# Turning batch 0's last three attention tiles on TensorE, and holding batch 1's first stacks behind tile 45

## The chip, the cores and the metric

The kernel runs on one core of a Trainium2 chip. The metric is device time in microseconds (us); the kernel before takes 764.54 us, the median of 3 runs (763.83 to 765.95). The engines are named as in the profile: PE (TensorE, its weight loads shown apart as PEld), DVE (VectorE), ACT (ScalarE), POOL (GpSimd) and SP (SyncE, which issues nearly all DMAs here).

## The reference

Three layers follow each other on a batch of 2, a sequence of 768 and a width of 512 (8 heads of 64).

```python
q_bucket, k_bucket = sums of 2**i over the signs of q @ proj, k @ proj   # 6 bits
scores = np.where(q_bucket == k_bucket, q @ k.T / 8, -1e9)
attn = softmax(scores) @ v                                # layer 1, per head
u = x + real(fft2(x)); un = (u - mean) / sqrt(var + 1e-6)
x = u + relu(un @ w_ch1) @ w_ch2                          # layer 2, hidden width 2048
theta = x @ w_theta
u = x + w_tok_r @ (x * cos(theta)) + w_tok_i @ (x * sin(theta))
out = u + relu(u @ w_ch)                                  # layer 3
```

## The kernel before

**Tiles.** Attention works on tiles of 128 queries by 768 keys. Each batch has 48 of them: 4 pairs of heads, 2 heads, 6 tiles of queries. For one tile PE makes the scores into PSUM (`pss`), DVE takes the row maximum (`nm`), ACT the exponential (`p`), then `p` is split into a high and a low half-precision part, turned so that keys lie on the partitions, and multiplied on PE with the values into `pso`. A head's six tiles done, DVE divides by the sums and writes the head's columns of `x` (the "norm").

**Two ways to turn a tile.** In way "d" POOL splits `p` (`attn_split`, L387) and a DMA transposes the parts (`transposed`, L410). In way "p" PE transposes the unsplit tile with six matmuls against the identity (`turn_pe`, L394), and ACT and DVE split it on the way out of PSUM (`split_turned`, L401: two ACT and two DVE instructions of 128x384). In batch 0 the two alternate, `pet='dp'`: even tiles go by "d", odd ones by "p".

**Order.** Batch 0's attention (`attention_first`, L472) is written out step by step: step n takes tile n's exponential, tile n+1's maximum, tile n-1's PE transposes and so on. While it is traced, `Ordered.keep` chains every instruction to the one before it on its engine; those instructions carry L64 in the profile. All others carry L62, and a list scheduler places them by priority, `at(us)`, and by its own estimate of time. Each engine then runs its list strictly in that order.

**What else runs.** `prep` (L235) makes a head pair's "stacks": it loads q, k and v (`tt`, `vr`), scales k on POOL, splits v (`vv`: an ACT copy, then DVE), splits q and k (`stk`: ACT copies, POOL differences, DMAs between partitions), and adds the bucket bits by two small matmuls, DVE signs and ACT copies. Beside attention, `conv16` (L173) turns w_ch1 (`w1h`, `w1l`) and w_ch2 (`w2h`, `w2l`) from 64-bit integers into two half-precision parts, 16 pieces each: a load into one of three buffers `r`, two ACT passes, one DVE pass, an ACT copy (high part), a POOL difference (low part). As batch 0's heads end, `fold` (L579) begins the Fourier transform on DVE and ACT (`fa`, `zraw`, `hl...`); `rest` finishes it on PE (`psm` from `ct`, `sn`, `dt`), `ln_first` (L725) normalizes its first two row tiles (`un`, turned on PE into `unT`), and the hidden layer of batch 0 starts (`mlp1`: `psm<-unT,w1h`; `mlp2`: `psm<-w2h,hh`), in three groups of 256 rows. Batch 1's attention (`attention`, L435) runs meanwhile; in it all tiles go by "d", with ACT or POOL for the high part. After its last head come batch 1's transform, norm and hidden layer, then layer 3 of both.

**Gates.** `after_gate` (L428) makes what is traced inside it stand behind a given instruction. The edge is one of order, on that instruction's own engine alone. `gate["p1"]` holds batch 1's first `prep`; in the kernel before it is the row maximum, on DVE, of tile `c1` = 32.

Of the kernel before, what the change touches and what calls it, by code (L numbers as in the profile page):

```python
# [70 lines left out]
def fused_kernel(ctx, tc, A, out):  # L71
    nc = tc.nc
    V, AC, PE, PL, SY = (Ordered(tc, e) for e in (nc.vector, nc.scalar, nc.tensor, nc.gpsimd, nc.sync))
# [13 lines left out]
    def stt(eng, out, in0, in1, op, scale=1.0):  # L87
# [5 lines left out]
    T = dict(  # L93
        pet='dp', dup=1, c2=0, c0=44, cx=0, wm=6, gf=1, o2=0, xs=1, sb=2, al=[['p', 2], ['p2', 3], ['pt', 3]], cs='v', g0=1,
        lg=[[0, 2], [2, 4], [4, 6]], ub=2, pace0=1.6, lead=60, f0=60.0, w1=60.0, w1s=1.0, b1=115, pace1=2.6,
        w2=100.0, w2s=1.0, m0=170.0, f1=190.0, th=240.0, m1=290.0, z0=330.0, wt=300.0, n1=16, k1=16, c1=32,
        ne=42, es=150, ld='ss', lc='s', ps=[[0, 3], [0, 5], [1, 0], [1, 5]])
    P3 = ((0, 0), (0, 1), (1, 0))

# [26 lines left out]
    def at(us):  # L126

        tc.cur_priority = int(1000 * us)
# [94 lines left out]
    gate, made = {}, {}  # L223
# [151 lines left out]
    def attn_max(ps):  # L375
        nm = mk(sm_p, [128, 1], F32, "nm")
        return nm, V.tensor_reduce(out=nm, in_=ps[:, :, 0:384], axis=AX.XY, op=ALU.max, negate=True)
# [94 lines left out]
    def attention_first(pace, after):  # L472

        x_t[0] = mk(x_p, [128, NT, DM], F32, "x")
        N = 8 * NT
        ps, nm, ex, p, p2, tp, pt, o = ({} for _ in range(8))
# [23 lines left out]
        nm[0], _ = attn_max(ps[0])  # L500
        for n in range(N + 7):
            at(pace * n)
            m, kind = n % 12, lambda i: T["pet"][i % 2] if 0 <= i < N else ""
            if n < N:
                scores(n + 1)
                p[n], e = attn_exp(ps.pop(n), nm[n])
# [3 lines left out]
            if n + 1 < N:  # L510
                nm[n + 1], x = attn_max(ps[n + 1])
                if n + 1 == T["c1"]:
                    gate["p1"] = [x]
                if n + 1 == T["c0"]:
                    gate["cv"] = [x, e]
            if n - 1 in tp:
# [241 lines left out]
    w1, w2 = {}, {}  # L758
# [129 lines left out]
    h1, l1, c1, c2 = (ev(k) for k in ("aapap", "p", "p", "p"))  # L888
# [4 lines left out]
    with after_gate("start"):  # L893
        ft0 = Fft(0, "left")

    attention_first(T["pace0"], lambda b, j: ft0.fold(PO[j]))
    al = [x for t in kept for x in one(t, *range(t.shape[1]))]
    for k, n in T["al"]:
# [206 lines left out]
```

## Time and profile before

| | |
|---|---|
| median of 3 runs | 764.54 us |
| profiled execution | 762.63 us |
| its span on the core | 760.9 us |
| PE busy, share of the span | 676.1 us, 89% |
| DVE / ACT / POOL busy | 444.2 / 400.0 / 370.5 us |

The profiled execution took 1.73 us more than its span, the time around the first and the last instruction, and 1.91 us less than the median of the runs. Times in the rows are microseconds from the start of the span. A row of the timeline gives start, length, engine, line, operation, output and input tiles with their shapes, how many instructions were merged into it, and in brackets how long the engine sat idle before it and what ended the wait. Names are without buffer numbers, so `w1h`, `w1l`, `p`, `pt` can be memory that a tile of attention borrows from the weights' room.

### The profile page before, as it was taken

How to read it: one execution, taken by the hardware profiler on the slowest of the kernel's cores; microseconds unless marked ns; L12 is line 12 of the kernel's file. 1: busy time of each engine (PE TensorE's matmuls, PEld its weight loads, DVE VectorE, ACT ScalarE, POOL GpSimd, SP SyncE). 2: the span in 40 equal slices, each digit the busy share in tenths (PEclk: the TensorE clock that was granted, in tenths of full speed). 3: DMA queues.
4: the chain of work that ended last, by engine and by line, in shares of the span. 5: the costliest groups of instructions: out<-in, count | busy, mean ns of one | idle time of the engine just before them, and what ended most of it. 6: DMA issues, size and time to landing. Idle time of an engine off the chain costs nothing.

```text
span 760.9 us, 14094 instructions
## 1 busy us (share of the span) xinstructions
PE 676.1 (89%) x5684; PEld 533.2 (70%) x5684; DVE 444.2 (58%) x728; ACT 400.0 (53%) x629; POOL 370.5 (49%) x296
## 2 busy tenths in 40 slices
PE   6978687778397898999989979999999998899997
PEld 2766566566295654786777666687584988899997
DVE  6778878698889755742395861154422496422222
ACT  4787596966597788773222161164325674730000
POOL 4786777896675888875460200033303378320000
PEclk7899996959599999999999989999999999799999
DMA  9675777678687999878640270020005612431100
GB/s 319 147 162 111 167 126 154 137 204 192 173 187 148 258 233 255 149 148 124 104 171 0 59 150 1 1 56 15 1 1 167 195 55 73 164 126 56 56 29 28
DMA packets 152641, 93.23 MB, mean 123 GB/s; under 512 B 126272, under 2 KB 138752, under 8 KB 152576
## 3 DMA queue, kind: packets, MB, share of 16 engines
q1 hardware_dynamic: 150704, 85.87, 48.5%
q0 software_dynamic: 1872, 6.47, 2.4%
q8 instruction: 44, 0.72, 0.4%
q14 instruction: 21, 0.17, 0.1%
HBM read 49.62 MB, written 6.29 MB: 73 GB/s over the span
## 4 chain that ended last, share of the span: by engine, by line
PE 44%; DVE 19%; DMA 11%; ACT 10%; issue 9%; POOL 7%; SPq 0%; POOLq 0%; ACTq 0%; DVEq 0%
PE psm L62 28%; PE psf L62 8%; DMA pt<-p 3%; PE pss L64 2%; ACT r L62 2%; DVE fa L64 2%; DVE nm L64 2%; DVE r L62 2%; DVE t L62 2%; PE pss L62 2%; DMA r<-in_wtok 2%; DMA r<-in_w 2%; DVE fa L62 1%; DVE rr L62 1%; ACT stk L64 1%
## 5 line engine op out<-in xcount | busy, mean ns | idle before, releaser
L62 PE MATMUL psm<-unT,w1h 128*128 128x256 f16 x768 | 131.9, 276 | 8.2 <-DMA unT<-u 4.8
L62 PE MATMUL psm<-unT,w1l 128*128 128x256 f16 x384 | 105.8, 276 | 0.0
L62 PEld LDWEIGHTS <-w1h 128*128 128x128 f16 (+1 forms) x774 | 75.6, 99 | 24.8 <-issue 12.1
L62 DVE SCALAR_TENSOR_TENSOR r<-r 128x512 uint32<-128x512 uint32 x58 | 57.6, 995 | 53.0 <-ACT r L62 48.2
L64 PE MATMUL pss<-stk 128*128 128x384 f32 x192 | 52.5, 397 | 23.6 <-ACT p L64 7.8
L62 PEld LDWEIGHTS <-hh 128*128 128x128 f16 x384 | 37.1, 99 | 43.1 <-issue 2.7
L62 DVE TENSOR_REDUCE nm<-pss 128x1 f32<-128x768 f32 x48 | 45.1, 950 | 34.6 <-PE pss L62 34.6
L62 ACT ACTIVATE r<-r,chalf 128x512 uint32<-128x512 uint32 x58 | 44.4, 766 | 35.7 <-DMA r<-in_wtok 16.7
L62 PE MATMUL psm<-w2l,hh 128*128 128x512 f16 x192 | 61.0, 383 | 0.0
L62 PE MATMUL psm<-w2h,hl 128*128 128x512 f16 x192 | 60.9, 382 | 0.0
L62 DVE SCALAR_TENSOR_TENSOR hl<-psm,hh 128x512 f16<-128x512 f32 x48 | 32.9, 687 | 47.8 <-ACT hh L62 47.7
L62 PE MATMUL psm<-w2h,hh 128*128 128x512 f16 x192 | 60.5, 382 | 0.0
L62 POOL TENSOR_TENSOR p<-p,p 128x768 f16<-128x768 f32 x32 | 54.3, 1703 | 11.7 <-ACT p L62 10.0
L62 POOL TENSOR_TENSOR w1l<-r,w1h 128x512 f16<-128x512 f32 (+1 forms) x28 | 35.3, 1271 | 49.3 <-ACT w1h L62 49.1
L62 ACT ACTIVATE p<-pss,nm 128x768 f32<-128x768 f32 x48 | 42.8, 896 | 29.4 <-DVE nm L62 28.7
L62 PE MATMUL pss<-stk 128*128 128x384 f32 x192 | 50.3, 388 | 8.8 <-ACT p L62 7.9
L62 ACT ACTIVATE hh<-psm 128x512 f16<-128x512 f32 x48 | 28.5, 593 | 51.8 <-PE psm L62 51.8
L64 PEld LDWEIGHTS pss<-stk 128*128 128x128 f32 x192 | 35.3, 212 | 28.9 <-ACT p L64 9.6
L64 DVE TENSOR_REDUCE nm<-pss 128x1 f32<-128x768 f32 x48 | 45.5, 950 | 15.3 <-PE pss L64 14.9
L62 PEld LDWEIGHTS pss<-stk 128*128 128x128 f32 x192 | 35.0, 206 | 13.4 <-ACT p L62 10.3
L62 PEld LDWEIGHTS <-w1l 128*128 128x128 f16 x384 | 38.0, 99 | 6.5 <-issue 1.8
L62 ACT ACTIVATE r<-r 128x512 f32<-128x512 f32 x58 | 38.5, 664 | 0.0
(279 smaller groups left out, 1807.0 us busy)
## 6 DMA issues: line engine op xcount, KB each, us to landing
r<-in_w SPq DMA_DIRECT2D x32, 512.0 KB, 4.4
r<-in_wtok SPq DMA_DIRECT2D x18, 512.0 KB, 4.8
stk<-stk SPq DMA_DIRECT2D x28, 192.0 KB, 3.2
vr<-in_v SPq DMA_DIRECT2D x8, 390.0 KB, 4.9
tt<-in_qT SPq DMA_DIRECT2D x8, 384.0 KB, 3.8
tt<-in_kT SPq DMA_DIRECT2D x8, 384.0 KB, 4.4
xT<-xs SPq DMA_DIRECT2D x12, 256.0 KB, 2.6
xt<-xT SPq DMA_DIRECT2D x6, 512.0 KB, 3.9
```

Of the source, the lines that this page charges most:

```text
L62: return fn(*a, **k)
L64: self.last = fn(*a, **k)
```

## The change

```diff
-        w2=100.0, ..., n1=16, k1=16, c1=32,
+        w2=100.0, ..., n1=16, k1=16, c1=45,
...
-            m, kind = n % 12, lambda i: T["pet"][i % 2] if 0 <= i < N else ""
+            m, kind = n % 12, lambda i: "" if not 0 <= i < N else "p" if i > N - 4 else T["pet"][i % 2]
...
                 if n + 1 == T["c1"]:
-                    gate["p1"] = [x]
+                    gate["p1"] = [e_.last for e_ in (V, AC, PL)]
```

With N = 48 the second edit makes tiles 45, 46 and 47 go by "p". Tiles 45 and 47 went that way already, so one tile changes, number 46: it loses POOL's two splits (128x768) and one DMA transpose, and gains six PE transposes, two ACT copies and two DVE subtractions of 128x384. The other two edits move the gate of batch 1's first `prep`. At step 44 the last instructions on the three engines are tile 45's row maximum on DVE, tile 44's exponential on ACT and tile 42's low split on POOL; what `prep` puts on DVE, ACT and POOL now stands behind them. SP and PE are not gated: the loads of `tt` stand where they stood.

The scheduler lays out all later instructions anew. Three places follow.

ACT, from tile 44 or 45 of batch 0 to its last tile: before, then after. `p`, `pt` and `w1l<-pss,nm` are exponentials, `w1l<-psm` and `w1h<-psm` the splits of tiles turned on PE, `stk<-tt` and `stk<-pss` batch 1's stacks, `w1h<-r` converted weights.

```order
L64 ACTIVATE p<-pss,nm 128x768 x2
L62 ACTIVATE stk<-tt 64x768 x2
L64 ACTIVATE w1l<-psm 128x384 x2
L64 ACTIVATE pt<-pss,nm 128x768
L62 ACTIVATE stk<-pss,hb 64x768 x4
L64 ACTIVATE w1l<-psm 128x384 x2
L62 ACTIVATE p<-pss,nm 128x768
L62 ACTIVATE p_113<-p 128x768
L62 ACTIVATE p<-pss,nm 128x768
L62 ACTIVATE w1h<-r_2039 128x512
```

```order
L62 ACTIVATE stk<-tt 64x768 x2
L64 ACTIVATE w1h<-psm 128x384 x2
L64 ACTIVATE p<-pss,nm 128x768 x2
L62 ACTIVATE stk<-tt 64x768 x2
L64 ACTIVATE w1l<-psm 128x384 x2
L64 ACTIVATE pt<-pss,nm 128x768
L64 ACTIVATE w1l<-psm 128x384 x2
L62 ACTIVATE stk<-pss,hb 64x768 x4
L62 ACTIVATE w1h<-r_2048 128x512
L62 ACTIVATE w1h<-r_2055 128x512
L62 ACTIVATE w1h<-r_2062 128x512
L64 ACTIVATE w1l<-psm 128x384 x2
```

The first head's `stk<-tt`, which stood before and after tile 41's exponential, with `vv` ahead of tile 40's, now stand behind tile 44's (`vv` just ahead of the first row). Tile 46's split is new, and three converted pieces have come ahead of tile 47's split, the last row.

DVE, in the fold of batch 0's third and fourth head pair: the two instructions of 128x4 that finish the column at the edge of `hle` leave their place among tiles 42 and 43 (first piece) and stand behind the last norm (second piece, of after).

```order
 L64 TENSOR_REDUCE nm<-pss 128x1
-L62 CAST hle<-fa 128x4
 L64 TENSOR_TENSOR zraw<-fa 128x384
-L62 TENSOR_TENSOR hle<-fa,hle 128x4
 L64 TENSOR_TENSOR hlz_187<-zraw,hlz_187 128x6x64
 L64 TENSOR_REDUCE nm<-pss 128x1
```

```order
L64 TENSOR_TENSOR zraw<-fa 128x256
L64 TENSOR_TENSOR hle<-zraw,hle 128x4x64
L64 CAST hle<-fa 128x4
L64 TENSOR_TENSOR hle<-fa,hle 128x4
L64 TENSOR_TENSOR zraw<-fa 128x192
```

They were filed among the tiles by priority; now they belong to the written order of the last fold.

DVE, at the end of batch 1's attention: `nm` are its last maxima, `hl` the low parts of batch 0's hidden layer, `r`, `x` the last norm, `fa` the fold that starts batch 1's transform.

```order
 L62 TENSOR_REDUCE nm<-pss 128x1 x3
 L62 SCALAR_TENSOR_TENSOR u<-psm,u 128x512 x2
-L62 SCALAR_TENSOR_TENSOR hl<-psm,hh 128x512 x2
-L62 TENSOR_SCALAR r<-pso 128x6
-L62 RECIPROCAL r<-r 128x6
-L62 TENSOR_TENSOR x<-pso,r 128x6x64
+L62 SCALAR_TENSOR_TENSOR hl<-psm,hh 128x512
+L62 TENSOR_SCALAR r<-pso 128x6
+L62 RECIPROCAL r<-r 128x6
+L62 TENSOR_TENSOR x<-pso,r 128x6x64
+L62 SCALAR_TENSOR_TENSOR hl<-psm,hh 128x512
```

The norm has moved one hidden-layer result ahead: on PE, less of batch 0's hidden layer stands in front of batch 1's last tile.

## Rows read from the trace of the kernel before

**Rows 1.** Busy time by stretch: the stretch, its length, then for PE, PEld, DVE, ACT and POOL the busy time with the count of instructions, the granted TensorE clock (1.00 is 2.4 GHz), the DMA share and GB/s.

```profile
110.00:150.00 40.00, 31.42 (x351) 25.12 (x349) 30.24 (x48) 31.47 (x50) 32.48 (x26) 0.83 0.71 145
150.00:184.00 34.00, 26.35 (x166) 21.51 (x166) 31.88 (x31) 23.10 (x39) 30.71 (x22) 0.70 0.79 195
184.00:206.00 22.00, 10.36 (x89) 7.38 (x87) 18.73 (x33) 14.00 (x20) 11.84 (x11) 0.68 0.70 186
243.00:306.00 63.00, 56.01 (x502) 35.88 (x503) 42.07 (x47) 51.86 (x77) 51.76 (x36) 0.95 1.05 240
306.00:371.00 65.00, 64.95 (x683) 47.39 (x681) 28.89 (x39) 36.43 (x48) 45.73 (x31) 1.00 0.80 132
```

**Rows 2.** The timeline at the end of batch 0's attention: tile 46's low split and DMA transpose, tile 47's split, the two last products with the values, the norm.

```profile
143.13 1.64 POOL L64 TENSOR_TENSOR w1h<-p,w1h 128x768 f16<-128x768 f32 x1
144.79 0.87 ACT L64 ACTIVATE w1l<-psm 128x384 f16<-128x384 f32 x2
144.80 1.43 SPq L64 DMA_TRANSPOSE w1l<-w1h  x1
145.63 1.15 PE L64 MATMUL pso<-vv,w1l 128*128 128x65 f16 x18
148.50 0.73 PE L64 MATMUL pso<-vv,w1l 128*128 128x65 f16 x18 [0.88 <-DMA w1l<-w1h]
149.27 0.17 DVE L64 TENSOR_SCALAR r<-pso 128x6 f32<-128x6 f32 x1 [0.65 <-PE pso L64]
149.69 0.56 DVE L64 TENSOR_TENSOR x<-pso,r 128x384 f32<-128x384 f32 x1
```

**Rows 3.** The timeline of ACT and DVE at tiles 41 and 42: batch 1's `stk` between the exponentials, tile 42's maximum and its exponential.

```profile
119.28 0.84 ACT L62 ACTIVATE stk<-tt 64x768 fp32r<-64x768 f32 x1 [2.02 <-DMA tt<-in_qT]
120.74 0.95 DVE L64 TENSOR_REDUCE nm<-pss 128x1 f32<-128x768 f32 x1
123.71 0.84 ACT L62 ACTIVATE stk<-tt 64x768 fp32r<-64x768 f32 x1 [2.80 <-POOL tt L62]
124.87 0.88 ACT L64 ACTIVATE pt<-pss,nm 128x768 f32<-128x768 f32 x1
```

**Rows 4.** The timeline of ACT: what is moved or added ahead of tile 47's split, as it ran before.

```profile
114.73 0.85 ACT L62 ACTIVATE vv<-vr 128x780 f16<-128x780 f32 x1
137.71 1.57 ACT L62 ACTIVATE stk<-tt 64x768 fp32r<-64x768 f32 x2
139.31 0.87 ACT L64 ACTIVATE w1l<-psm 128x384 f16<-128x384 f32 x2
148.63 1.79 ACT L62 ACTIVATE w1h<-r 128x512 f16<-128x512 f32 x3 [0.38 <-DMA w1l<-w1h]
```

**Rows 5.** Waits from 110 to 306 us: engine and tile, what it waited for, total us, times, longest.

```profile
ACT unT L62 <- PE psm L62: 5.3, 1, 5.3
DVE nm L62 <- PE pss L62: 13.7, 8, 3.5
DVE r L62 <- ACT r L62: 12.3, 8, 2.9
```

**Rows 6.** The timeline of PE at the first two row tiles of `ln_first` and at the hidden layer's first product.

```profile
207.97 1.12 PE L62 MATMUL psm<-ident,un 128*128 128x128 f32 x4 [5.68 <-DVE un L62]
217.37 0.38 PE L62 MATMUL psm<-unT,w1h 128*128 128x256 f16 x2
```

**Rows 7.** Groups of like instructions over the whole run: count, busy us, mean ns of one, idle time before them.

```profile
L62 ACT ACTIVATE r<-r,chalf 128x512 uint32<-128x512 uint32 x58 | 44.4, 766 | 35.7 <-DMA r<-in_wtok 16.7 <-DMA r<-in_w 9.6 <-DMA r<-in_wch 9.2
L62 ACT ACTIVATE p<-pss,nm 128x768 f32<-128x768 f32 x48 | 42.8, 896 | 29.4 <-DVE nm L62 28.7 <-POOL p L62 0.6
L62 ACT ACTIVATE r<-r 128x512 f32<-128x512 f32 x58 | 38.5, 664 | 0.0
L62 ACT ACTIVATE p<-p 128x768 f16<-128x768 f32 x20 | 16.6, 837 | 1.0 <-DMA pt<-p 0.9
L62 ACT ACTIVATE w1h<-r 128x512 f16<-128x512 f32 x16 | 10.5, 665 | 6.8 <-DVE r L62 6.4 <-DMA w1l<-w1h 0.4
L62 DVE SCALAR_TENSOR_TENSOR r<-r 128x512 uint32<-128x512 uint32 x58 | 57.6, 995 | 53.0 <-ACT r L62 48.2 <-issue 3.5 <-POOL w2l L62 0.6
L62 DVE TENSOR_REDUCE nm<-pss 128x1 f32<-128x768 f32 x48 | 45.1, 950 | 34.6 <-PE pss L62 34.6
L64 DVE TENSOR_TENSOR w1l<-psm,w1l 128x384 f16<-128x384 f32 x24 | 12.2, 548 | 0.8 <-ACT w1l L64 0.7
```

**Rows 8.** The timeline of DVE: the two 128x4 instructions that change place.

```profile
121.60 0.92 DVE L62 CAST hle<-fa 128x4 fp32r<-128x4 f32 x1
122.91 0.78 DVE L62 TENSOR_TENSOR hle<-fa,hle 128x4 fp32r<-128x4 f32 x1
```

**Rows 9.** The timeline of DVE and PE: the maxima of tiles 30 and 48 of batch 1, and two neighbouring products of `mlp2`, whose starts give the step.

```profile
306.37 0.94 DVE L62 TENSOR_REDUCE nm<-pss 128x1 f32<-128x768 f32 x1
370.54 0.96 DVE L62 TENSOR_REDUCE nm<-pss 128x1 f32<-128x768 f32 x1 [5.17 <-PE pss L62]
398.37 0.38 PE L62 MATMUL psm<-w2h,hl 128*128 128x512 f16 x1
398.58 0.38 PE L62 MATMUL psm<-w2h,hh 128*128 128x512 f16 x1
```

**Rows 10.** PE's waits from 371 to 446 us: the longest.

```profile
PE psm L62 <- DMA unT<-u: 4.8, 1, 4.8
```

**Rows 11.** The instructions on two tiles: count, then the shortest, median and longest time in ns. `r` is DVE's pass over a converted piece (both inputs in SBUF), `hl` has one input in PSUM.

```profile
L62 DVE SCALAR_TENSOR_TENSOR r<-r x58: 673/694/2793, 131.3 to 674.3; 128x512 uint32<-128x512 uint32 x58
L62 DVE SCALAR_TENSOR_TENSOR hl<-psm,hh x48: 671/691/693, 225.1 to 570.5; 128x512 f16<-128x512 f32 x48
```

More of the change, by code (lines that the diff above doesn't have):

```diff
@@ L95, in fused_kernel @@
         lg=[[0, 2], [2, 4], [4, 6]], ub=2, pace0=1.6, lead=60, f0=60.0, w1=60.0, w1s=1.0, b1=115, pace1=2.6,
-        w2=100.0, w2s=1.0, m0=170.0, f1=190.0, th=240.0, m1=290.0, z0=330.0, wt=300.0, n1=16, k1=16, c1=32,
+        w2=100.0, w2s=1.0, m0=170.0, f1=190.0, th=240.0, m1=290.0, z0=330.0, wt=300.0, n1=16, k1=16, c1=45,
         ne=42, es=150, ld='ss', lc='s', ps=[[0, 3], [0, 5], [1, 0], [1, 5]])
```

## The prediction

> **What bounds the kernel now.** I read the table of stretches first. From 306 to 371 us PE is busy 64.95 of 65 us: there batch 1's attention and batch 0's hidden layer share a full engine. Before that no engine is full: PE is busy 10.36 of 22 us from 184 to 206, a trough in which POOL and ACT idle too, at a granted clock of 0.68, and from 243 to 306 it is ACT and POOL that are busiest after PE, with 51.86 and 51.76 of 63 [rows 1]. So up to 306 us the kernel is a weave of in-order lists that wait for each other, and what an early edit is worth depends on whether it still shows at 306 us, where PE takes over and passes every microsecond on. Second, the timeline at the change: batch 0's attention ends with tile 46, whose POOL split ran from 143.13 and whose DMA transpose was issued at 144.80 and let PE go at 148.50, while tile 47's product, by PE transposes, had ended at 146.78 (145.63 + 1.15). The norm began at 149.27 [rows 2]. Third, the waits: two of the longest single ones are ACT's 5.3 us for the first `unT`, and PE's 5.68 for `un` [rows 5, 6].
>
> **The change part by part, on the profiled execution's 762.63 us.**
>
> *Batch 0's last tiles (term A).* Removed: batch 1's `stk` copies between tiles 41 and 42. ACT idled 2.02 us ahead of one and 2.80 ahead of the other, with the next exponential queued behind: tile 42's maximum ended at 121.69 (120.74 + 0.95), its exponential started at 124.87, 3.18 us late [rows 3]. That is what tiles 42 to 44 gain, since tile 43's and 44's steps hang on it one by one: 3.2. It is given back on ACT. Ahead of tile 47's split now stand `vv` with 0.85, two `stk` copies with 1.57, tile 46's own split with 0.87 and three converted pieces with 1.79, in all 5.1 us [rows 4]. So tile 47's product, which ended at 146.78, ends at 146.78 - 3.2 + 5.1 = 148.7, and with tile 46 no longer behind a DMA the norm begins there instead of at 149.27 [rows 2]: -0.6. Tile 46's POOL split and its transpose thus save little: another queue ends 0.6 us sooner. Its six transposes on PE and two subtractions on DVE lie beside ACT's queue there. Bounds: -2.5, if the 5.1 us fall into gaps of ACT's (the norm at 146.78), and +2.5, if tile 44 gains nothing (151.9). What follows on POOL: four stack differences and a scaling of k come behind tile 44's split and so wait no more for the loads; the loads themselves stay in SP's list where they were, and cost nothing new.
>
> *From the norm to tile 30 of batch 1 (term B).* In the new order 16 more ACT instructions stand ahead of the first `unT` copy: four pairs of conversion passes, 4 x (0.766 + 0.664) = 5.7; two high parts of weights, 1.3; one exponential and one high part of a tile, 1.7; two `stk` copies, 1.6 (two of 1.57 [rows 4]); tile 46's split, 0.9; together 11.2. On DVE six more stand ahead of the first `un`: two conversions, two maxima and two subtractions, 2.0 + 1.9 + 1.1 = 5.0 [rows 7]. So `un` comes about 5 us later and the hidden layer's first product goes from 217.37 [rows 6] to some 222, while ACT's wait of 5.3 us [rows 5] is filled with 11.2 us of work that needs doing anyway. The late start is covered: `mlp2` of the first group needs w_ch2, whose pieces are converted until about tile 30. Ahead of tile 30's scores, PE's list has the same 216 products of `mlp1` and 96 of `mlp2` in both orders, and DVE's 34 conversions instead of 33. What counts is when tile 30 is reached, 306.37 before [rows 9]. If ACT sets that pace, its wait of 5.3 is gained less the split of 0.9 that is new: -4.4. If DVE does, nothing goes but the two `hle` instructions of 0.92 and 0.78 [rows 8] come into its queue behind the norm, where they delay the transform: +1.7. DVE's own waits are for ACT (12.3 us) and for PE's scores (13.7) [rows 5], which speaks for ACT; DVE's 31.88 of 34 us from 150 to 184 [rows 1] speaks for DVE. I take the middle, -1.4.
>
> *From tile 30 to batch 1's transform (term C).* Here PE is full [rows 1]. Ahead of tile 48's scores, 176 products of `mlp2` stand instead of 185. Their step is 0.21 to 0.22 us (398.37 to 398.58): nine are 1.9 us, so tile 48, at 370.54 before, comes 1.9 us sooner relative to tile 30 [rows 9]. The nine are then done while batch 1's transform and norm run on DVE, where PE stood idle 4.8 us for `unT` at the end [rows 10] and so has room for them. Batch 1's hidden layer starts 1.9 us sooner. Bounds: -1.9 and 0, the latter if the tiles wait for their transposes rather than for PE. Behind it, the order of layer 3 is all but unchanged; I cost it at nothing.
>
> *Sum:* -0.6 - 1.4 - 1.9 = -3.9, so 758.7 for an execution like the profiled one. That one lies 1.9 below the median of the runs, 764.54, so against the runs I forecast 760.6 us.
>
> **A rule against the change.** DVE's pass over a converted piece takes 694 ns in the median but up to 2793, while `hl`, with one input in PSUM, never leaves 671 to 693 [rows 11]; the mean over 58 is 995 [rows 7], 0.3 us above the median each time. The Trainium skill, page "SBUF — State Buffer", section "Who interferes with whom", says that a DVE instruction with two SBUF inputs contends with a GpSimd instruction that reads SBUF, and that whichever comes second blocks until the first is done. The trace agrees (2793 against 694 ns). By it, work that moves on POOL toward the transform makes DVE's queue there longer than its own instructions say; this is the first rival's mechanism.
>
> **The rivals.**
>
> *DVE sets the pace and POOL holds it (slower).* Place: DVE between the norm and the first `un`, 149.69 to 207.97. Batch 1's four stack differences and tiles 1 and 2's splits now run on POOL closer to the fold. DVE has 5.0 us more ahead of `un`, and each moved POOL instruction can hold a two-input one by up to 2.1 (2.793 - 0.694): two such holds on the path are 4.2. For it: DVE's 31.88 of 34 us. Against: the same work is done before tile 30 in either order, and most of the 5.0 us is work taken from later. Price: A at 0, B at +1.7 + 4.2 = +5.9, C at -1.9, in all +4.0: 768.5 against the runs. It decides from the point where tile 30's maximum comes more than 2 us later than 306.37.
>
> *ACT sets the pace alone.* For it: 11.2 us of ACT's work go into a trough, and ACT is busy 51.86 of 63 us after it. Against: POOL is as busy, 51.76 [rows 1]. A at -2.5, B at -4.4, C at -1.9: -8.8, 755.7 against the runs.
>
> *It levels out.* By tile 22 the two orders have converted the same 26 pieces and made the same eight `hl`; if tile 30 is reached when it was and the tiles behind it wait for DMA transposes, A and B cancel and C is 0. What is left is the norm's 0.6: 763.9.
>
> *The gate holds less than its words say.* It binds neither SP nor PE; if the stacks' start were set by the loads alone, ACT's order would not matter for tiles 45 to 47 and A would stay within its bounds. That is inside the forecast's range, so it gets no chance of its own.
>
> **How the numbers follow.** The forecast (-1.5 to -6) gets 0.35, ACT alone 0.16, levelling out 0.27, DVE and POOL 0.22. A measurement of this kernel can tell about 0.3% from no change, 2.3 us. Faster: 0.32 of the forecast's 0.35, the 0.16, and 0.02 of the levelling cases, 0.50. Slower: the 0.22 but 0.02 of it, and 0.03 of levelling cases on the far side, 0.23. The rest, 0.27, is the same. The range for 8 in 10 goes from 755.0, a little past ACT alone, to 768.5, the slower rival's price. The forecast's own range is 758.5 to 763.
>
> **What would show it.** Right: tile 47's split on ACT ends last in batch 0 and the norm begins near 148.7; no DMA ends PE's last wait there; ACT no longer waits 5 us for the first `unT`; the first `mlp1` product comes some 5 us later, at about 222, and tile 30's maximum nevertheless 1 to 3 us sooner, near 304.4; from tile 30 to tile 48 it takes about 62 instead of 64.2 us; PE's last wait before batch 1's hidden layer is under 4.8 us. Wrong: a norm after 150, ACT waiting as long as before in other places, tile 30 at or after 306.4, or a difference that first appears behind 443 us, in layer 3, which I took as unchanged.

## The result, and the profile after

The changed kernel takes 775.13 us (median of 4 runs, 772.44 to 776.71), the kernel before 764.18 (4 runs beside them, 763.0 to 765.95): a ratio of 1.0135, with a 95% interval of 1.011 to 1.016. It is slower by 10 to 11 us where 3.9 us of gain were forecast, and beyond the range's upper end of 768.5. The profiled execution took 775.4 us with a span of 773.62 (before 762.63 and 760.86), so the two traces differ by 12.8.

Four marks divide that: batch 0's last norm (`x` on DVE, 149.69 before [rows 2], 152.49 now), tile 30's maximum of batch 1 (306.37 [rows 9], now 321.19), tile 48's (370.54 [rows 9], now 386.66), and the end.

| stretch | before | after | difference | predicted |
|---|---|---|---|---|
| to the norm | 149.69 | 152.49 | +2.8 | -0.6 |
| norm to tile 30 | 156.68 | 168.70 | +12.0 | -1.4 |
| tile 30 to tile 48 | 64.17 | 65.47 | +1.3 | -1.9 |
| tile 48 to the end | 390.32 | 386.96 | -3.4 | 0 |

So the loss sits between the norm and tile 30, and most of it ahead of the first `un`: that begins 66.42 us behind the norm instead of 56.26. First the busy time of both parts, norm to `un` and `un` to tile 30 (columns as in [rows 1]), of before:

```profile
149.69:205.95 56.26, 37.02 (x253) 28.89 (x251) 50.87 (x63) 37.41 (x60) 42.85 (x31) 0.69 0.76 192
205.95:306.37 100.42, 86.54 (x798) 62.89 (x799) 76.95 (x116) 81.71 (x121) 75.61 (x53) 0.93 0.95 216
```

and of after:

```profile
152.49:218.91 66.42, 33.80 (x279) 27.24 (x278) 58.80 (x70) 46.55 (x74) 55.81 (x38) 0.76 0.80 196
218.91:321.19 102.28, 92.85 (x793) 67.60 (x794) 71.52 (x114) 73.78 (x109) 67.39 (x48) 0.86 0.88 191
```

Up to `un`, DVE has 70 instructions instead of 63, is busy 7.9 us longer (58.80 against 50.87), and fills 58.80 of 66.42 us: of the 10.2 us more, DVE's busy time is 7.9. PE idles 32.6 us (66.42 - 33.80) where it idled 19.2. Behind `un`, PE has 793 matmul records up to tile 30 instead of 798 (the list has the same 216 products of `mlp1` and 96 of `mlp2` ahead of it), yet is busy 6.3 us longer for them, at a mean clock of 0.86 instead of 0.93. The two maxima that end and begin this part, in DVE's timeline of after:

```profile
321.19 0.94 DVE L62 TENSOR_REDUCE nm<-pss 128x1 f32<-128x768 f32 x1
386.66 0.96 DVE L62 TENSOR_REDUCE nm<-pss 128x1 f32<-128x768 f32 x1 [5.20 <-PE pss L62]
```

Two waits are two thirds of PE's 32.6 us of idle time. The timeline of PE in after shows them, and what runs behind the second (in brackets: idle before, and what ended it):

```profile
166.30 1.01 PE L62 MATMUL psm<-ct,hlz 128*128 128x386 f32 x2 [12.27 <-ACT hlz L64]
...
219.51 1.12 PE L62 MATMUL psm<-ident,un 128*128 128x128 f32 x4 [8.98 <-DVE un L62]
...
222.08 3.44 PE L62 MATMUL psm<-dt,fa 128*128 128x128 f32 x15
...
232.89 0.65 PE L62 MATMUL psm<-unT,w1h 128*128 128x256 f16 x2
```

The same steps before, beside [rows 6]:

```profile
159.10 1.01 PE L62 MATMUL psm<-ct,hlz 128*128 128x386 f32 x2 [3.51 <-ACT hlz L64]
...
210.87 2.62 PE L62 MATMUL psm<-dt,fa 128*128 128x128 f32 x15
```

The wait for `hlz` grew from 3.51 to 12.27, that for `un` from 5.68 [rows 6] to 8.98, and the transform's 15 products behind it took 3.44 instead of 2.62. The table of stretches has the clock: in after, 0.52 and then 0.51, about the lower level of 1.2 GHz, through the wait and 16 us beyond it; before, 0.80 in the 16 us from 206.

```profile
207.00:219.00 12.00, 1.54 (x21) 1.05 (x19) 11.72 (x14) 6.97 (x11) 11.43 (x8) 0.52 1.09 257
219.00:235.00 16.00, 15.03 (x80) 13.12 (x81) 8.39 (x16) 7.33 (x11) 3.97 (x3) 0.51 0.67 132
```

The row of before:

```profile
206.00:222.00 16.00, 14.03 (x139) 13.07 (x140) 13.46 (x26) 12.79 (x19) 9.80 (x7) 0.80 0.72 176
```

What DVE does while PE waits is in its timeline. From the norm to the first `zraw`, from which `hlz` is made, after has:

```profile
152.49 0.56 DVE L64 TENSOR_TENSOR x<-pso,r 128x384 f32<-128x384 f32 x1
152.97 0.95 DVE L62 TENSOR_REDUCE nm<-pss 128x1 f32<-128x768 f32 x1
153.83 2.94 DVE L64 TENSOR_TENSOR fa<-x 128x384 f32<-128x384 f32 x2
156.69 0.94 DVE L62 TENSOR_REDUCE nm<-pss 128x1 f32<-128x768 f32 x1
157.56 1.62 DVE L62 SCALAR_TENSOR_TENSOR vv<-vr,vv 128x780 f16<-128x780 f32 x1
159.10 1.21 DVE L64 TENSOR_TENSOR fa<-fa 128x384 f32<-128x384 f32 x1
160.24 2.12 DVE L62 SCALAR_TENSOR_TENSOR r<-r 128x512 uint32<-128x512 uint32 x1
162.28 1.99 DVE L64 TENSOR_TENSOR fa<-fa 128x384 f32<-128x384 f32 x1
164.31 1.39 DVE L64 TENSOR_TENSOR zraw<-fa 128x384 f32<-128x384 f32 x1
```

Line 64 (batch 0) makes the chain for which PE waits; line 62 is batch 1's and the weights' work. Between the links stand a second maximum (0.94) and a converted piece (2.12, held), neither of which was there before; `zraw` comes 11.8 us behind the norm instead of 7.7. Shortly before `un`, DVE's and POOL's timelines of after have to be read side by side. DVE's:

```profile
207.72 1.55 DVE L62 TENSOR_TENSOR t<-rs,ve 128x2 f32<-128x2 f32 x1
209.31 0.75 DVE L62 SCALAR_TENSOR_TENSOR t<-t,rs 128x2 f32<-128x2 f32 x1
210.09 0.16 DVE L62 SCALAR_TENSOR_TENSOR rs<-t,rs 128x2 f32<-128x2 f32 x1
210.29 1.66 DVE L62 TENSOR_TENSOR t<-rs,ve 128x2 f32<-128x2 f32 x1
...
217.12 1.56 DVE L62 SCALAR_TENSOR_TENSOR t<-t,rs 128x2 f32<-128x2 f32 x1
```

POOL's at the same two moments:

```profile
207.61 1.64 POOL L62 TENSOR_TENSOR p<-p,p 128x768 f16<-128x768 f32 x1
...
217.01 1.65 POOL L62 TENSOR_TENSOR p<-p,p 128x768 f16<-128x768 f32 x1
```

An instruction on 128x2 numbers takes 0.16 us when free. The one at 207.72 ends at 209.27, POOL's subtraction at 209.25; the one at 217.12 ends at 218.68, POOL's at 218.66. They end when POOL ends. I call the excess of an instruction over the shortest time of the same operation on the same tiles, in any trace of this document, its hold, and add up all durations less these shortest ones from the norm to `un`: 23.5 us over 63 instructions before, 27.5 over 70 in after. The shortest times themselves add up to 30.8 and 35.1 us.

### The profile page after: what moved, and what is told of

Its sections match the earlier page's. It is cut to its first block, busy times and chain, and to the rows that moved or that the text cites. A ratio compares the mean times of both kernels' runs of the same rounds, so it can differ in the third digit from the quotient of the medians.

```text
span 773.6 us, 14095 instructions
## 1 busy us (share of the span) xinstructions
PE 677.1 (88%) x5690; PEld 534.1 (69%) x5690; DVE 444.8 (57%) x730; ACT 400.8 (52%) x631; POOL 369.5 (48%) x294
## 4 chain that ended last, share of the span: by engine, by line
PE 47%; DVE 20%; ACT 9%; issue 9%; DMA 8%; POOL 5%; SPq 1%; ACTq 0%; DVEq 0%; POOLq 0%
PE psm L62 30%; PE psf L62 8%; DVE t L62 3%; PE pss L62 2%; PE pss L64 2%; DMA r<-in_w 2%; DVE fa L64 2%; DVE nm L64 2%; PE psm L64 2%; ACT r L62 2%; DVE rr L62 1%; PE pso L64 1%; PE pso L62 1%; ACT stk L64 1%; POOL p L62 1%
## 5 line engine op out<-in xcount | busy, mean ns | idle before, releaser
L62 PE MATMUL psm<-unT,w1h 128*128 128x256 f16 x768 | 135.4, 280 | 4.5 <-DMA unT<-u 3.3
L62 PE MATMUL psm<-unT,w1l 128*128 128x256 f16 x384 | 107.4, 280 | 0.0
L62 PEld LDWEIGHTS <-w1h 128*128 128x128 f16 (+1 forms) x774 | 76.8, 101 | 21.8 <-issue 9.7
L62 DVE SCALAR_TENSOR_TENSOR r<-r 128x512 uint32<-128x512 uint32 x58 | 48.6, 840 | 57.3 <-ACT r L62 51.5
L64 PE MATMUL pss<-stk 128*128 128x384 f32 x192 | 51.0, 387 | 26.3 <-ACT p L64 6.7
L62 ACT ACTIVATE p<-pss,nm 128x768 f32<-128x768 f32 x48 | 42.7, 895 | 36.4 <-DVE nm L62 23.5
L62 POOL TENSOR_TENSOR w1l<-r,w1h 128x512 f16<-128x512 f32 (+1 forms) x28 | 37.7, 1363 | 46.3 <-ACT w1h L62 46.3
L62 PE MATMUL pss<-stk 128*128 128x384 f32 x192 | 49.1, 382 | 6.3 <-ACT p L62 6.2
```

Of the source, the lines that this page charges most:

```text
L62: return fn(*a, **k)
L64: self.last = fn(*a, **k)
```

## The experiments

Four causes were weighed against each other: the lists' counts (what stands ahead of `zraw` and `un` in DVE's in-order queue), POOL's holds, PE's clock behind its waits, and, as the rival to all three, that the loss belongs to one part of the change (tile 46's transposes, or the gate) whatever stands in the queues. The table gives each run's median and ratio, and of its profiled execution (up to 3.8 us off the median) the start of the norm's `x`, how far behind it the first `zraw` came, the starts of `un` and of tile 30's maximum, and PE's idle time from `x` to `un`. Diffs are against the changed kernel unless "before" is said.

| run | median us | ratio, 95% interval | norm | zraw | un | tile 30 | PE idle |
|---|---|---|---|---|---|---|---|
| before | 764.18 | 1 | 149.7 | +7.7 | 206.0 | 306.4 | 19.2 |
| after | 775.13 | 1.0135 [1.011, 1.016] | 152.5 | +11.8 | 218.9 | 321.2 | 32.6 |
| e1 transposes alone | 768.79 | 1.0047 [1.0017, 1.0076] | 155.9 | +7.8 | 217.0 | 312.4 | 24.1 |
| e2 gate alone | 765.23 | 1.0011 [0.9986, 1.0036] | 152.1 | +10.5 | 205.8 | 313.2 | 20.8 |
| e3 gate at tile 43 | 778.15 | 1.0146 [1.0098, 1.0195] | 155.2 | +7.8 | 219.3 | 326.0 | 25.9 |
| e4 gate on POOL alone | 770.16 | 1.0055 [1.0032, 1.0078] | 155.8 | +7.5 | 211.7 | 316.1 | 22.6 |
| e5 before, 3 steps more | 768.38 | 1.0054 [1.003, 1.0077] | 154.0 | +7.7 | 216.2 | 317.3 | 23.2 |
| e6 one step less | 774.17 | 1.0135 [1.0101, 1.0169] | 151.8 | +9.1 | 216.4 | 319.0 | 28.5 |
| e7 fewer tiles and pieces ahead | 771.18 | 1.0078 [1.0045, 1.011] | 151.7 | +11.6 | 209.6 | 322.0 | 21.5 |
| e8 fewer tiles ahead | 773.80 | 1.0122 [1.0094, 1.0151] | 151.9 | +11.4 | 214.7 | 322.2 | 25.4 |
| e9 fold first | 764.55 | 1.0008 [0.9984, 1.0033] | 152.8 | +6.8 | 214.0 | 309.6 | 21.8 |
| e10 POOL without reads | 761.12 | 0.9956 [0.9936, 0.9977] | 150.9 | +9.6 | 205.8 | 300.7 | 16.1 |
| e11 before, one step less | 766.69 | 1.0033 [1.0008, 1.0058] | 150.6 | +7.7 | 202.1 | 317.0 | 16.8 |
| e12 e7 and e9 together | 767.59 | 1.0043 [1.0023, 1.0063] | 152.9 | +7.2 | 210.2 | 314.7 | 20.1 |
| e13 pieces alone behind the fold | 766.57 | 1.0024 [1.0, 1.0047] | 151.3 | +10.8 | 214.9 | 320.5 | 24.7 |
| e14 empty products, two places | 765.34 | 1.002 [0.9995, 1.0045] | 153.9 | +7.7 | 211.3 | 310.1 | 13.9 |
| e15 gate alone, fold first | 767.81 | 1.0043 [1.0021, 1.0066] | 152.9 | +6.9 | 209.4 | 319.0 | 22.4 |
| e16 before, fold first | 769.64 | 1.0062 [1.0034, 1.009] | 151.8 | +6.6 | 207.4 | 315.2 | 19.5 |
| e17 empty products ahead of `un` | 764.15 | 1.0004 [0.9982, 1.0025] | 151.7 | +11.5 | 210.6 | 314.1 | 18.5 |
| e18 gate on ACT alone | 772.71 | 1.0093 [1.0059, 1.0126] | 152.0 | +11.4 | 216.4 | 318.1 | 25.8 |

The marks come from one execution each, and two executions of one order differ. e18 has after's lists, entry for entry, on PE, DVE and ACT, and on POOL but for two neighbours; yet its `un` is 2.5 us sooner, its tile 30 3.1 us, and the sum of its holds is 23.4 us, not 27.5. e5 has the lists of before on every engine until shortly before `un`, and its norm is 4.3 us later. e6 has after's list from the norm to `zraw`, and needs 9.1 us for it instead of 11.8. So 2 to 4 us between two single marks show nothing by themselves. In e14 and e17 the empty products count as busy; without them PE idles 21.2 and 23.3 us.

Of the times expected below, those of the reading that I favoured were missed on the slow side by e3, e4 and e11 and on the fast side by e9, e14 and e17.

Tile 30's place can be compared only where PE's list has like counts of `mlp1` ahead of it: in after, e1, e9, e10, e14 and e18 it has 216 to 232 by that time, in e6, e7, e8, e13, e15 and e17 over 255.

**The parts of the change (e1 to e4, e18).** e1 keeps the transposes and puts the gate back; e2 keeps the gate and gives tile 46 its DMA back.

```diff
-                    gate["p1"] = [e_.last for e_ in (V, AC, PL)]
+                    gate["p1"] = [x]
-        w2=100.0, ..., c1=45,
+        w2=100.0, ..., c1=32,
```

> Batch 0's last three tiles by PE transposes, batch 1's first stacks as before (behind tile 32). Theory Q (DVE's queue between the norm and the first un sets the time, held by POOL, and a late un is passed on one for one): ahead of the first un stand 66 DVE instructions from the norm on with 40.7 us of own work, against 63 with 38.5 before and 70 with 44.5 after; at the 1.4 us of busy time per us of own work that both traces show, un comes 3 us later and the kernel takes about 767 us. Rival N (the norm, late because batch 1's stack copies stand behind tile 44's exponential on ACT, carries everything): no loss, 764. Rival K (tile 46's new kind, with the turned ring of buffers, carries it): nearly the whole loss, 772 to 775.

```diff
-            m, kind = n % 12, lambda i: "" if not 0 <= i < N else "p" if i > N - 4 else T["pet"][i % 2]
+            m, kind = n % 12, lambda i: T["pet"][i % 2] if 0 <= i < N else ""
```

> The gate of after (tile 45, three engines), tile 46 by POOL and DMA as before. Q: only 60 DVE instructions with 37.4 us from the norm to the first un, 1.1 us less than before, so un 1.5 us sooner after the norm; the norm itself late by the 2.8 us that after shows; about 765.5. N: the stacks stand behind tile 44's exponential as in after, so most of the loss is here, 770 or more. K: no loss, 764.

The transposes alone cost 0.5%, the gate alone nothing that can be told, together 1.35%: by the medians the parts don't add up, by the outer ends of their intervals (0.76 + 0.36 against 1.1) they just might. In e1 the norm is latest of all (155.9) and the time only 4.4 us over the 764.39 of before in that comparison, so a late norm is not the loss. In e2 the gate's order has DVE's `zraw` late too (+10.5), but `un` at 205.8 as before. So the costly thing seems to need both; e1 has a late `un` (217.0) too, for a third of the price.

e3 moves the gate to tile 43 (`c1=43`), e4 and e18 leave one engine's entry in it.

> As after, but the gate opens at tile 43 instead of 45: 64 DVE instructions with 39.1 us from the norm to the first un. Q: 0.6 us more own work than before, +0.8 us, and a norm up to 1 us later: 765 to 766. N: between before and after, 768 to 772. K: 772 to 775.

```diff
-                    gate["p1"] = [e_.last for e_ in (V, AC, PL)]
+                    gate["p1"] = [PL.last]
```

> As after, but the gate at tile 45 waits for POOL's last instruction alone, not for ACT's and DVE's: 63 DVE instructions with 38.1 us from the norm to the first un. Q: 0.4 us less own work than before, -0.6 us, and the norm's place: 763 to 766. N: 764 if the stacks are not behind tile 44's exponential, up to 775 if they are. K: 772 to 775.

e18 has `[AC.last]` in that place.

> The kernel after with ACT's last instruction alone in the gate instead of three engines' last ones; it moves two neighbouring instructions on POOL and nothing else. If ACT's entry is the one that holds: the time of after, 773 to 777. If DVE's or POOL's matters on the chip: 768 or less.

e3 is as slow as after with only 64 instructions ahead of `un`, not 70, and `zraw` at +7.8: here DVE itself waits 11.7 us in all (after 7.6), mostly for ACT and PE. A count of DVE's queue by itself does not predict the time. With POOL's entry alone the loss falls to 0.55%; with ACT's alone it stays (0.93%, an interval that overlaps after's), though `un` is 2.5 us sooner than in after. Since its lists are after's, e18 is in effect a second measurement of after: ACT's entry is the one that orders the lists, and the other two add nothing.

**The length of DVE's queue ahead of `un` (e5 to e8, e11).** The Newton steps for 1/sqrt of the first row tiles' variance stand on DVE just ahead of `un`; e5 gives the kernel before three more, e11 one less, e6 the changed one one less (the lines are those of e6 and e11; e5 has 6 in place of 2).

```diff
-        for _ in range(3):
+        for _ in range(2 if not b and not g[0] else 3):
```

> The kernel before, with six instead of three steps of the iteration for the first group's reciprocal root: nine more small DVE instructions straight ahead of the first un, at 0.16 us each where nothing holds them and up to 1.8 where POOL does (1.5 to 16 us), and two maxima that slip in. Theory U (a late first un is handed on one for one): un 4 to 10 us later than 205.95, tile 30, tile 48 and the end later by as much: 768 to 774. Rival C (a late un is covered, as the prediction had it; the tiles' own steps set the pace): un as late, but tile 30 within 2 us of 306.4 and the time 763 to 766.

> The kernel after, with two instead of three steps for the first group (a lower precision of that root): three small DVE instructions fewer ahead of un, which took 1.10, 1.56 and 0.16 us, all else ahead of un as in after. U: un 2 to 4 us sooner than 218.91 and the time 771 to 773. C: un as much sooner, the time still 775.

> The kernel before, with two instead of three steps of the iteration for the first group's reciprocal root (a lower precision of that root): the three instructions ahead of the first un that took 1.06, 1.57 and 0.76 us are gone, all else ahead of un as before. Theory P: un 2 to 3.4 us sooner, time 761 to 763. C: un as much sooner, time 764.

e5 brings `un` 10 us later than before, but 4.3 of them stand at the norm already, where the steps can have no part. From the norm it is 5.9 us later (62.20 us against 56.26), with the nine small instructions and two maxima more, and costs 0.54%, 4 us, where after's 10.2 us cost 1.35%, 10 us. So e5 leaves open whether a late `un` is passed on for the most part. e6 gains 2.5 us at `un`, no more than e18 with nothing taken away, and nothing in the end. e11 is slower than before although `un` comes 3.8 us sooner: the planner put other work into PE's list behind it, and PE idles there for `hl` (8.1 us in two waits). Every run that changes counts also changes the planned order.

e8 lets batch 1's tiles wait for the transform from tile 10 on (`n1=10`), e7 from tile 9 on and converts three pieces less ahead (`n1=9, k1=13`).

> The kernel after, but batch 1's tiles from the 9th (not the 16th) and the conversions from the 13th (not the 16th) wait for the first unT: ahead of un 65 DVE instructions from the norm on with 40.2 us of own work (after 70 with 44.5, before 63 with 38.5). Theory Q: 4.3 us of own work less, at 1.4 busy per own some 6 us: un near 213, and with U the time near 769. C: un sooner, but the three tiles and two pieces that now come behind it cost as much there: 773 to 777.

> The kernel after, but batch 1's tiles from the 10th wait for the first unT: two maxima of 0.95 us fewer ahead of un (68 instructions, 42.6 us). Q and U: un 2 to 3 us sooner, time 772 to 773. C: 774 to 776.

e7 has `un` 9.3 us sooner and is 4 us faster than after, not 9; e8 gains 1.3 (within the intervals). Both leave `zraw` at +11.4 to +11.6, so PE's first long wait stays.

**What stands between norm and `zraw` (e9, e12, e13).** e9 lets batch 1's exponentials from tile 2 on (counted from 0), and all conversions but three, begin behind batch 0's first `zraw`.

```diff
-                    with after_gate(0 if b and n >= T["n1"] else None):
+                    with after_gate(0 if b and n >= T["n1"] else "fold" if b and n >= 2 else None):
-            V.tensor_tensor(out=r, in0=a, in1=b, op=op)
+            gate.setdefault("fold" if len(self.done) == 4 and not self.b else "x", V.tensor_tensor(out=r, in0=a, in1=b, op=op))
-        timed(take(cw1, T["k1"]), T["w1"], T["w1s"])
+        timed(take(cw1, 3), T["w1"], T["w1s"])
+    with after_gate("fold"):
+        timed(take(cw1, T["k1"] - 3), T["w1"] + 3, T["w1s"])
```

> The kernel after, but batch 1's tiles from the 3rd and the conversions from the 4th piece wait for the first `zraw`, so that on DVE two maxima and one converted piece leave the stretch between the last norm and the first `zraw` (0.94, 0.94 and 2.12 us there) and come right behind it. Theory P (what the change loses is PE's idle time between the norm and the first un, 32.6 against 19.2 us, of which 12.3 stand ahead of the transform's first product): zraw 8 us behind the norm instead of 11.8, PE's long wait 8 to 9 us instead of 12.3, time 770 to 772. Rival C (PE's idle time there is made up later): the wait shorter, the time still 774 to 776.

The whole loss is gone: 1.0008, with both parts of the change in place. DVE's timeline now has the chain without the two maxima and the piece, and PE's wait for `hlz` is 6.41:

```profile
153.37 2.05 DVE L64 TENSOR_TENSOR fa<-x 128x384 f32<-128x384 f32 x2
155.34 1.91 DVE L62 SCALAR_TENSOR_TENSOR vv<-vr,vv 128x780 f16<-128x780 f32 x1
157.17 2.38 DVE L64 TENSOR_TENSOR fa<-fa 128x384 f32<-128x384 f32 x2
159.58 1.10 DVE L64 TENSOR_TENSOR zraw<-fa 128x384 f32<-128x384 f32 x1
```

From norm to `un` and on to tile 30:

```profile
152.77:213.98 61.21, 39.37 (x262) 31.00 (x260) 53.73 (x69) 42.21 (x67) 46.13 (x33) 0.67 0.77 191
213.98:309.57 95.59, 86.50 (x774) 63.41 (x774) 70.18 (x114) 76.68 (x113) 72.61 (x51) 0.91 0.94 217
```

`un` is still 8 us later than before, but the stretch behind it is 4.8 us shorter than before's (95.59 against 100.42), with PE busy 86.50 as before (over 774 matmul records instead of 798). This is the cover on which the prediction counted: work done ahead of `un` can come back by tile 30. In after it does not: the stretch takes 102.28 us, and 101.68 in e18 with the same lists.

e13 puts only the conversions behind the fold; e12 has the edits of e7 and e9 together.

> The kernel after, but only the conversions from the 4th piece wait for the first `zraw`: one piece (2.12 us) leaves DVE's stretch between norm and first `zraw`, the two maxima (0.94 each) stay. If the piece is the cause: zraw 8.5 to 9.7 us behind the norm, time 765 to 769. If it takes the maxima too, or their later place: zraw as far behind, but time 771 to 775.

> The kernel after with both remedies: tiles from the 3rd and pieces from the 4th behind the first `zraw`, tiles from the 9th and pieces from the 13th behind the first unT (65 DVE instructions with 40.2 us from the norm to un). P: PE's idle time between norm and un falls from 32.6 to some 18 to 22 us and the time to 764 to 768. C: 771, as with the second remedy alone.

e13 takes most of the loss away with `zraw` still at +10.8 and so doesn't settle whether the maximum or the piece matters more; its PE list is another one too (259 products of `mlp1` by tile 30). e12 has `un` 3.8 us sooner than e9 and is 3 us slower by the medians, with intervals that overlap: remedies don't add up either.

**POOL's holds (e10).** POOL's subtractions for pieces 4 to 16 and for batch 1's first 14 tiles become two fills each, of similar length.

```diff
-            stt(lo_eng(i), lo[:, c], w, hi[:, c], ALU.subtract)
+            if lo is w1.get(1) and 2 < i < 16:
+                for _ in range(2):
+                    PL.memset(lo[:, c], 0.0)
+            else:
+                stt(lo_eng(i), lo[:, c], w, hi[:, c], ALU.subtract)
```

> The kernel after, but POOL's low parts of the conversion's pieces 4 to 16 and of batch 1's first 14 tiles are two fills with zero instead of a subtraction of two tiles in SBUF (those low parts are left out of the result). DVE has the same 70 instructions with 44.5 us of own work between the norm and un. Theory H (POOL's passes over SBUF hold DVE's there: 27.5 us above the shortest time of each form): the excess falls to 10 to 15 us, un comes 8 to 15 us sooner, the time 762 to 768. Rival (those long times are DVE's own, whatever POOL does): excess 25 to 30 us, un at 215 to 219, time 773 to 776.

DVE has the same 70 instructions ahead of `un`, and the sum of their holds falls from 27.5 to 13.4 us. The last steps ahead of `un` run free:

```profile
205.40 0.16 DVE L62 SCALAR_TENSOR_TENSOR t<-t,rs 128x2 f32<-128x2 f32 x1
205.60 0.16 DVE L62 SCALAR_TENSOR_TENSOR rs<-t,rs 128x2 f32<-128x2 f32 x1
205.80 1.00 DVE L62 TENSOR_SCALAR un<-u,mv,rs 128x512 f32<-128x512 f32 x2
```

`un` is 13.1 us sooner than in after, and the kernel beats before by 0.44%. This is no usable version, since the low parts are missing. And it is not clean: PE's list ahead of `hlz` changed as well, POOL is busy 39.8 us from the norm to `un` instead of 55.8, and two of its stack subtractions came behind `un` (see e17), so its 14 us are not all the holds' price. What it shows is that the same DVE instructions carry half the excess when these passes of POOL only write. That is as the rule of the Trainium skill that the prediction quoted has it (page "SBUF — State Buffer", section "Who interferes with whom").

**PE's clock (e14, e17).** e14 fills PE's two waits with 20 and 16 products whose results nobody reads; e17 puts 24 such products ahead of `un`'s transposes, started by `ve`.

```diff
+                if not self.b and nm == "z2" and cos:
+                    with tc.issue_after(gate["pe"].ins):
+                        for _ in range(20):
+                            mm(ps[:, 0:n], ct[:, 0, 0, 0:128], ct[:, 0, 0], True, True)
```

> The kernel after with 36 empty products on PE (20 ahead of the transform's first product, where PE waited 12.3 us, and 16 behind the transform's last product of the first group, where it waited 1.8 to 3.8 us); their results are overwritten. DVE's work ahead of un is 69 instructions with 43.5 us, after 70 with 44.5. Theory K (the clock: after PE's long waits the products up to tile 30 run partly at half the clock and take 92.9 us of PE's time instead of 86.6): the granted clock from un to 235 us rises from 0.51 to 0.8 or more, the time falls by 3 to 6 us, 769 to 772. Rival (the late un alone): clock higher, time 774 to 777.

```diff
+        for _ in range(24):
+            mm(pt0[0:2, 0:128], gate["warm"], ident, True, True)
```

> The kernel after with 24 empty products of 128 columns on PE that need the first group's variance (`ve`), right ahead of the first un's transposes, in the stretch in which PE waited 9.0 us; DVE and ACT have the same instructions in the same order up to the last four ahead of un. Theory K (the clock eats what should come back behind un): the granted clock from 207 to 235 us is 0.7 or more instead of 0.51, un at 216 to 220, from un to tile 30 some 97 to 99 us instead of 102.3, time 769 to 772. Rival (the late un alone): clock as high, time 774 to 777.

e17's stretches, against 0.52 and 0.51 in after:

```profile
207.00:219.00 12.00, 10.64 (x95) 8.50 (x92) 10.48 (x20) 7.99 (x13) 7.04 (x6) 0.92 0.90 199
219.00:235.00 16.00, 13.53 (x154) 11.58 (x153) 15.61 (x42) 9.09 (x13) 9.44 (x7) 1.00 0.72 212
```

The clock is up and the loss is gone, with `zraw` as late as in after (+11.5) and PE's wait for `hlz` at 11.29: so that first wait alone is not the loss. But `un` came 8.3 us sooner as well. Of DVE's instructions only one maximum had moved behind it. What else moved are two `stk` copies on ACT and the two subtractions on POOL that need them, which in after run beside the Newton steps; POOL's timeline of after, then of e17:

```profile
210.14 4.08 POOL L62 TENSOR_TENSOR stk<-tt,stk 64x768 fp32r<-64x768 f32 x2
```

```profile
223.68 3.71 POOL L62 TENSOR_TENSOR stk<-tt,stk 64x768 fp32r<-64x768 f32 x2 [5.95 <-ACT stk L62]
```

The nine instructions of the three steps take 9.6 us in after and 1.4 in e17 (before 4.5), and the sum of the holds is 18.1 us instead of 27.5. e14 likewise has this pair behind `un`, and took `zraw` to +7.7. So both say that an execution with PE kept busy there loses nothing, and neither tells the clock from the lateness.

e18 helps, for the stretch behind `un`. In the 16 us from the end of PE's wait its granted clock was 0.76, in after 0.53 (219.51 to 235.51). Its stretch from `un` to tile 30:

```profile
216.42:318.10 101.68, 88.92 (x791) 64.33 (x791) 72.75 (x114) 73.84 (x109) 68.71 (x49) 0.90 0.92 196
```

For the same products PE is busy 3.9 us less than in after, and idle 3.3 us more: the stretch is 0.6 us shorter. In this pair the lower clock mostly took time in which PE would have waited anyway.

**Is it the order as such? (e15, e16).** e9's lines in e2 and in the kernel before.

> The gate alone (tile 46 as before), with tiles from the 3rd and pieces from the 4th behind the first `zraw`: 60 DVE instructions with 37.4 us from the norm to un, none of batch 1's in front of the first `zraw` but one subtraction of v. The gate alone measured 1.0011 of before. If the stretch to the first `zraw` (10.5 us there) is worth in this kernel what it was worth in after: 3 to 8 us less, 757 to 762. If the gate alone has no such loss to give back: 763 to 766.

> The kernel before, with tiles from the 3rd and pieces from the 4th behind the first `zraw`: one maximum of 0.95 us leaves the 7.7 us from the norm to the first `zraw`, and another slips in ahead of un. At one for one: 763 to 764; if the order behind it matters more than that microsecond, anything from 758 to 772.

e16 is 0.6% slower than the kernel before; e15 0.3% slower than e2 by the medians, with intervals that overlap. The remedy helps only where the change has done its harm; around the order of before, each of e5, e11 and e16 costs 0.3 to 0.6%, one of them with work taken away.

## Why the prediction was wrong

**Term A (-0.6 forecast, +2.8 measured).** The gain at tiles 42 to 44 was there but smaller: tile 43's to 45's maxima come 2.1, 2.5 and 1.8 us sooner (tile 44's: 127.95 after 130.42), not 3.2, and tile 46's is 0.5 later: on ACT `vv` and two copies now stand ahead of tile 45's exponential, which starts at 135.53 instead of 135.00. ACT's timeline ahead of tile 47's split in after:

```profile
143.36 0.87 ACT L64 ACTIVATE w1l<-psm 128x384 f16<-128x384 f32 x2 [1.77 <-PE psm L64]
144.61 3.63 ACT L62 ACTIVATE stk<-pss,hb 64x768 fp32r<-64x768 f32 x4 [0.38 <-PE pss L62]
148.27 1.75 ACT L62 ACTIVATE w1h<-r 128x512 f16<-128x512 f32 x3
150.04 0.87 ACT L64 ACTIVATE w1l<-psm 128x384 f16<-128x384 f32 x2
```

The steps forecast are there (tile 46's own split, three pieces with 1.75), and tile 47's split ends last, as said. But it begins at 150.04 instead of 144.79 [rows 2], 5.3 later, with the 3.2 that should have come off all but gone and a wait of 1.77 for tile 46's transposes, which the sum had "beside ACT's queue". So the place was right and the wait left out. The net size can't be told from this pair of traces, though 2.8 stands just outside the bound of +2.5 (2.6 by its own terms, 151.88 - 149.27): three traces with the order of before have the norm at 149.7, 150.6 (e11) and 154.0 (e5), ten with after's order up to there at 151.3 to 153.9, 152.2 in the mean.

**Term B (-1.4 forecast, +12.0 measured): the step that failed.** "The late start is covered" and "I take the middle", between ACT and DVE as the pace. Up to `un` DVE sets it, busy 58.80 of 66.42 us, and behind `un` nothing is covered: the stretch to tile 30 is 1.9 us longer than before, 1.3 in e18. The 5.0 us more ahead of `un` were right in kind (seven instructions against six: three maxima, two pieces, the two `hle`; 4.3 us of shortest times), and ACT's wait for `unT` did shrink, from 5.3 [rows 5] to 3.52 only. But `un` came 10.2 us later behind the norm, since the sum had the instructions at their own length alone: some 4 us more are holds in after's trace and some 2 are waits of DVE's (in e18, 8.2 us later, no more hold than before, but 4 us more of waits). `mlp1` began at 232.89, not 222. The sum did not speak of PE's first wait either, for `hlz` (12.27 against 3.51); but e17 and e13 keep that wait (11.29 and 9.78) and lose nothing and 0.24%, so it is not the loss by itself. Nor is the clock behind the second wait: PE's 6.3 us more were 2.4 in e18, at nearly the same length of the stretch. Why the lateness comes back in e9 (95.59 us from `un` to tile 30) and not in after stays open.

The two `hle` instructions, costed at +1.7 for a DVE that sets the pace, took 0.16 and 0.17 us in after: they were held before [rows 8], and weren't now.

**Term C (-1.9 forecast, +1.3 measured).** Its other bound, that tiles wait for their transposes rather than for PE, is what happened, and past it. From tile 30's maximum to tile 48's, by the table of stretches, of before:

```profile
306.37:370.54 64.17, 64.12 (x677) 46.83 (x676) 28.06 (x38) 36.06 (x47) 45.36 (x31) 1.00 0.77 131
```

and of after:

```profile
321.19:386.66 65.47, 61.22 (x653) 45.41 (x653) 24.18 (x36) 35.22 (x45) 43.38 (x30) 0.97 0.73 123
```

PE does have less to do there (61.22 instead of 64.12), but idles 4.25 us, where it idled 0.05; its one long wait is for a DMA transpose of a p tile:

```profile
PE pso L62 <- DMA pt<-pt: 3.5, 1, 3.5
```

"PE is full" was true of the order of before, not of after's. Behind tile 48 after is 3.4 us shorter, so that the two together come to -2.1, near the forecast by another way than forecast; PE's last wait ahead of batch 1's hidden layer, forecast under 4.8 [rows 10], was 3.3.

**The rivals.** "DVE sets the pace and POOL holds it" named the mechanism and the place, and its point of decision was met (tile 30 at 321.19, more than 2 us past 306.37). Its price of +4.0 was about a third of what came, because it took the 5.0 us as given back later: with them, 5.0 + 4.2 = 9.2, it would have come near `un`'s delay, 10.2, though the holds' 4.0 of after's trace are not there in e18's. It was given 0.22; DVE's 31.88 of 34 us [rows 1] and the pieces of up to 2793 ns [rows 11] spoke for more. "ACT alone" and "It levels out" fell with tile 30. Of the signs to look for, no DMA ended PE's last wait at the norm, as forecast, and the norm at 152.5 and tile 30 past 306.4 were both on the list of what would prove it wrong.

**What the runs bear out.** In the changed kernel and its variants the time goes roughly with PE's idle time from norm to `un`: 32.6 us of it at 775.1, 25 to 29 at 773 to 774 (e6, e8, e18), 20 to 22 at 764 to 768 (e9, e12), 16.1 at 761.1 (e10). e3 (25.9 at 778.2), e7 (21.5 at 771.2), e13 (24.7 at 766.6) and e17 (23.3 without its empty products, at 764.2) lie off it. Around the kernel before it doesn't hold (e11, 16.8 at 766.7). Another sign separates the runs better: where POOL's two stack subtractions stand that e17 moved. In the seven traces that have them ahead of `un` (after, e1, e3, e5, e6, e8, e18) the kernels take 768.4 to 778.2 us, in the other thirteen 761.1 to 771.2. No run moved them by themselves, and in e9 and e13 `un` is late without them, so this is a sign and not a cause shown.

I read the chain so: the gate on ACT and the missing DMA wait of tile 46 bring batch 1's maxima, pieces and stacks forward into the transform's chain and the Newton steps on DVE; DVE's queue, held by POOL, makes PE wait twice; and behind the waits PE doesn't catch up. That the work brought forward makes the loss is borne out by e9, which holds maxima and pieces back behind the fold and has the time of before; e9 moved other entries with them, and which of them weighs is not shown. POOL's part is borne out by e10 and e17, with the reservations made there. The clock's part was small where one list was measured twice (after and e18). Whether the maximum, the piece or the stack subtractions are worse stays open. No version that computes everything beat before: e9 and e17 equal it.

## What to carry to other kernels

Ask of each engine with an in-order list what stands between the links of the chain that the largest engine waits for: work that has slack, put there by a gate that frees it all at once, costs the wait, and the large engine need not make it up behind it. Price small instructions on SBUF at their held time wherever GpSimd is busy beside them (0.16 us free, up to 1.76 held, here; the copy `lone<-u` of 128x2, with one input, took 1.60 in after). Measure one order twice before reading a shift of a mark: 2 to 4 us between two traces were nothing here. An order that a planner's table settles looks like a picked one: here six of seven small edits around it (e1, e4, e5, e11, e15, e16; not e2) cost 0.3 to 0.6% whatever they meant, so an edit's own merit can only be read beside its re-plan.

## What was not expected of the hardware

Two of DVE's 128x2 instructions ended within 0.02 us of POOL's subtraction beside them; with fills in place of POOL's subtractions the sum of the holds over 70 instructions fell from 27.5 to 13.4 us. And behind PE's wait of 8.98 us the granted clock was 0.51 for 16 us of nearly full work (15.03 of 16 us), where 24 products without use in that wait had it at 1.00 in e17. In e18, with the same lists and a wait of 9.00, it was 0.50 for 6 us and 0.92 in the ten behind them: when the clock came back differed between two executions of one order, and the time from `un` to tile 30 followed it by 0.6 us only.
